# A convolution and a hard-swish layer on one core: the last convolution tap one unit earlier, a level-two sum moved from VectorE to GpSimd, and four ScalarE steps re-timed

## The chip, the core and the metric

The kernel runs on one core of a Trainium2 chip. The core has five engines that run their own instruction streams and wait for one another through semaphores: TensorE (PE in the profile; its weight loads are PEld), VectorE (DVE), ScalarE (ACT), GpSimd (POOL) and SyncE (SP), which here only issues DMAs. GpSimd issues DMAs as well, among them those that add to what is at the target. The metric is the device time of one execution in microseconds, and the time of the kernel before is the median of three runs.

## The reference

What is computed is a short causal convolution and, on its result, a two-layer network with a hard-swish between the layers, all in fp32:

```python
w = exp(weight - max(weight)); w = w / (sum(w) + 1e-9)      # (8 heads, 7 taps)
out = einsum('hk,bskhg->bshg', w, x_unf)                    # x: (8, 4096, 192), 7 taps back in time
x = out.reshape(32768, 192)
h = x @ w_in                                                # (192, 2048)
g = h * clip(h + 3.0, 0.0, 6.0) / 6.0
return g @ w_out                                            # (2048, 192)
```

## The kernel before

**Blocks.** The 32768 tokens are worked off in 32 blocks of 1024, each in two groups of 512. Block 0 is done in another way while the weights are prepared; blocks 1 to 31 are alike, and each runs `first_layer` (lines 499 to 570) and then `second_layer` (623 to 911). The last block differs a little: it has no convolution to prepare, and its output is finished in halves.

**The first layer.** The product with w_in is made from three parts (HIGH, LOW, MIX) of the operands, each rounded to a faster matmul format. There are 16 units n: 8 chunks of the 2048 inner columns for each of two groups. A unit takes one of four slots of two PSUM banks. `begin(n)` issues the HIGH and LOW matmuls, 12 of them, and ScalarE multiplies the slot by 4097 (L523; for unit 15 one half is done by ScalarE in L526 and the other by VectorE in L527). `end(n)` issues the 6 MIX matmuls, ScalarE makes the clipped factor (L302, "gate input") and VectorE multiplies it with the slot into the tile g (L306, "gate"). Then the slot is free: the HIGH matmuls of unit n + 4 wait for the gate of unit n. The order on TensorE is end(n), begin(n + 2), except that begin(15) stands before end(13). Two matmuls run side by side in the upper and the lower half of the array.

**Work between the units.** `jobs` puts work on VectorE behind given units, the taps of the convolution for the next block among it (L1053, one of 7 taps over 128 x 1536 elements; five of them fall here). The tile x is read by these taps alone, so that the load of the next one (L82 and L83, SyncE's queue, in the program behind the first layer) waits for the last tap.

**The second layer** multiplies g, as a 2 x 2 matrix of blocks A11, A12, A21, A22, by w_out with seven products in place of eight. The sums that it needs are written over the blocks or into the tile S3 (`s` in the profile):

| name | what | made by | where |
|---|---|---|---|
| S3 | A11 - A21, in pairs of chunks 0 to 3 | "third sum": GpSimd for pairs 0 and 1, VectorE for 2 and 3 | L414, S3 |
| S1 | A21 + A22, in the same pairs | `add_pair`: accumulating DMA on GpSimd's queue, behind its third sum | L573, over A21 |
| S2 | S1 - A11 | VectorE, half at a time | L414, over A11 |
| S4 | A12 - S2, in four pairs | `negative`: ScalarE writes -S2 (L576), a DMA of GpSimd's queue adds A12 | over S3 |

For the last 32 of the 96 output columns, products 1, 5, 2 and 4 are themselves split in the same manner ("level two", `small` products 1 to 7). The sums for these are made by `small_sums` (L605): `shared` from A11, `sums4` from A22 (z in the profile, which names other tiles of that kind z too), `sums2` from A12 and s5 from S1. Sum 3 is a difference of two blocks, sum 2 takes sum 3, and sum 4 takes sum 2. The first of each is made by a copying DMA (L556, L559) and an accumulating one.

**What sets the order.** TensorE's work in the second layer is written as four streams, one for each quarter of the array's columns, which run side by side. Each matmul gets a step of its stream's clock: a plain one of 512 tokens costs two steps, one of 256 tokens (level two) one, and each stream is 80 steps long. Copies, sums and DMAs for the other engines are given due times with `do(t, ...)`, put at t - 0.5. All are sorted by time and issued in that order; ties keep the order of the code. TensorE executes strictly in order, so that a matmul of one stream that waits holds all four. Stream 3 begins with product 1's level two, and at step 4 `fill(2)` brings the first two chunks of product 5, which read S1's first pair. Stream 2 has product 4's level two (`level_two(4, ...)`, order 1, then 6, 2, 7, 5, 4, 3) with chunks of product 7 ("c7", T3 times S3) in between. The level-two results are held in pieces of PSUM with names: A2, E2, C2, B2, D2 for product 2, and `chains` for the others; between two products that build on one another ScalarE copies a piece (L745 to L750, and L814 to L824 by due time; a copy called through `do` shows as L652). `fold` adds the pieces on VectorE.

Of the kernel before, what the change touches and what calls it, by code (L numbers as in the profile page):

```python
# [25 lines left out]
def kernel(  # L26
# [8 lines left out]
    nc = tc.nc  # L35
# [19 lines left out]
    NP = NC // 2  # L55
# [32 lines left out]
    for base, dma in ((0, nc.scalar), (D2, nc.sync)):  # L88
        dma.dma_start(
            out=w_sb[base : base + D2],  # L90
            in_=weight.unsqueeze(1).to_broadcast([H, GJ, KC]),
# [126 lines left out]
    for n in range(AHEAD):  # L218
# [8 lines left out]
        out=e_sb[:], in0=w_sb[:], in1=mx[:].to_broadcast([P, KC]), op=ALU.subtract  # L227
# [46 lines left out]
    A11, A21, A12, A22 = (g4[:, :, j] for j in range(4))  # L274
# [26 lines left out]
    def relu(r6, h):  # L301
        nc.scalar.activation(r6, h, ACT.Relu, bias=half[:], scale=1.0 / 6.0)  # L302

    def gate(g_, h):

        nc.vector.scalar_tensor_tensor(  # L306
            out=g_, in0=g_, scalar=1.0, in1=h, op0=ALU.min, op1=ALU.mult
        )
# [46 lines left out]
    every = range(NP)  # L355
# [90 lines left out]
    def rows(q):  # L446
        return slice(q * QS, (q + 1) * QS)
# [24 lines left out]
    def r32(ap):  # L472
        return ap.bitcast(F32R)
# [16 lines left out]
    y_own, y_other, pools, sums4 = [], [None], [], []  # L490
# [8 lines left out]
    def first_layer(i, jobs):  # L499

        slots = {}

        def both(n):
            return psum[:, 2 * slots[n] : 2 * slots[n] + 2]

        def mms(n, part, start=False, stop=False):
            group, c = divmod(n, NP)
            for s in range(K3):
                for k in range(2):
                    r = slice(k * D2, (k + 1) * D2)  # L510
                    nc.tensor.matmul(  # L511
                        out=psum[:, 2 * slots[n] + k], lhsT=r32(w_in_parts[part][r, c, s]),
                        rhs=r32(y_other[0][r, part, s] if group else y_own[part][r, s]),
                        start=start and s == 0, stop=stop and s == K3 - 1,
                        skip_group_check=True,
                    )

        def begin(n):
            slots[n] = free_slots.pop(0)
            mms(n, HIGH, start=True)  # L520
            mms(n, LOW)
            if n + 1 < count:
                nc.scalar.mul(both(n), both(n), 4097.0)  # L523
            else:
                lower, upper = (psum[:, 2 * slots[n] + k] for k in range(2))
                nc.scalar.mul(lower, lower, 4097.0)  # L526
                nc.vector.tensor_scalar(  # L527
                    out=upper, in0=upper, scalar1=4097.0, scalar2=None, op0=ALU.mult
                )

        def end(n):
            group, c = divmod(n, NP)
            mms(n, MIX, stop=True)
            to = g4[:, c, 1:3] if group else g4[:, c, 0::3]
            relu(to, both(n))
            gate(to, both(n))
            free_slots.append(slots[n])

        count = 2 * NP
        begin(0)  # L540
        begin(1)
        for job in jobs.get(-1, ()):
            job()
        for n in range(count):
            if n == count - 3:
                begin(n + 2)
            end(n)
            if n < count - 3:
                begin(n + 2)
            for job in jobs.get(n, ()):  # L550
                job()
            if n < NP and n % 2:
                small_sums(shared, A11, (3, 2, 4), nc.gpsimd, every[n - 1 : n + 1])
            if n in (3, NP - 1):
                r = slice(n - 3, n + 1)
                nc.sync.dma_start(out=four_parts(shared[:, r])[0], in_=four_parts(A11[:, r])[2])  # L556
            if n == NP - 1:
                sums4[:] = [pools[0].tile([P, NP, N], F32, name="z4", tag="own")]
                nc.sync.dma_start(out=four_parts(sums4[0])[0], in_=four_parts(A22)[2])  # L559
                small_sums(sums4[0], A22, (3,), nc.gpsimd)  # L560
                adding(four_parts(shared)[0], four_parts(A11)[3])
            if n == NP + 1:
                third_sum(0)
                add_pair(0)
                adding(four_parts(sums4[0])[0], four_parts(A22)[3])
            if n == NP + 2:
                small_sums(sums4[0], A22, (2,), nc.vector)
            if n == NP + 3:
                third_sum(1)
                add_pair(1)  # L570

    def adding(out, x):
        nc.gpsimd.dma_start(out=out, in_=x, accum_op=ALU.add)  # L573
# [5 lines left out]
    def pair_of(p):  # L579
        return slice(2 * p, 2 * p + 2)  # L580

    def third_sum(p, engine=nc.gpsimd):
        g_sums(engine, (3,), every[pair_of(p)], 2)

    def add_pair(p):
        adding(S1[:, pair_of(p)], A22[:, pair_of(p)])
# [4 lines left out]
    def four_parts(x):  # L591
        return [x[:, c::2, t] for t in halves for c in range(2)]

    def small_sums(to, x, which, engine=nc.gpsimd, r=every):

        r = slice(r[0], r[-1] + 1)
        x11, x12, x21, x22 = four_parts(x[:, r])
        s1, s2, s3, s4 = four_parts(to[:, r])
        forms = {
            1: (s1, x21, x22, ALU.add), 2: (s2, x22, s3, ALU.subtract),  # L600
            3: (s3, x11, x21, ALU.subtract), 4: (s4, x12, s2, ALU.subtract),
        }
        for n in which:
            o, p, q, op = forms[n]
            engine.tensor_tensor(out=o, in0=p, in1=q, op=op)  # L605
# [17 lines left out]
    def second_layer(i, between):  # L623
        last = i + 1 == NB
        ours = [free_slots.pop(0) for _ in range(3)]
        x_, b, y_, c, a, _ = (psum[:, 2 * n + k] for n in ours for k in range(2))
# [4 lines left out]
        copy = nc.scalar.copy  # L631
# [3 lines left out]
        first, second, third, fourth = (rows(q) for q in range(4))  # L635
# [5 lines left out]
        A2, E2, C2, B2, D2 = f[first, lo], f[second, hi], h[first, lo], h[second, hi], h[third, hi]  # L641
# [5 lines left out]
        def put(j, cost, fn):  # L647
            streams[j].append((clock[j], fn))
            clock[j] += cost

        def do(t, fn, *args, **kw):
            streams[3].append((t - 0.5, lambda: fn(*args, **kw)))  # L652
# [7 lines left out]
        def plain(j, bank, n, q, chunks, start=False):  # L660
            x, w = prod[n]
            x = S3 if x is None else x
            for k, ch in enumerate(chunks):
                put(j, 2, lambda ch=ch, k=k: matmul(
                    j, bank[rows(j)], w_out[:, ch, w, q * QS : (q + 1) * QS], x[:, ch],
                    start and k == 0,
                ))
# [57 lines left out]
        def p2(r, t):  # L725
            return late["p2"][r, t]
# [13 lines left out]
        p4 = Fourth()  # L740
# [50 lines left out]
        p3(1)  # L791

        level_two(4, lambda: p4, (1,), 2)
        plain(2, c, 7, 2, every[:2], True)
        level_two(4, lambda: p4, rest, 2)
        plain(2, c, 7, 2, every[2:])
        plain(2, b, 6, 2, every)
        small(2, 3, D2, False, 2)
        p3(2)
# [15 lines left out]
            do(20 if t == hi else 16, copy, out=p4[third, t], in_=b[first, t])  # L815
        do(16, copy, out=p1[third], in_=b[second])
        do(20, copy, out=B2, in_=A2)
        do(32, copy, out=C2, in_=B2)
        do(32.2, copy, out=D2, in_=B2)
        do(32, copy, out=a[fourth], in_=a[second])  # L820
        do(40, lambda: copy(out=p2(second, hi), in_=C2))
        do(48, copy, out=a[second], in_=a[fourth])
        do(44, lambda: copy(out=p2(first, lo), in_=A2))
# [15 lines left out]
        do(32, fold_with, p1)  # L839
        do(35, small_sums, s5, S1, (3, 2), nc.vector)  # L840
        do(35.5, g_sums, nc.vector, (2,), every[4:], 4)
        do(32.5, fold_with, p4, 2)
        do(36, copy, out=b[m], in_=p1)
        do(21, last_sum, sums2, A12)
        do(36, small_sums, s5, S1, (1, 4), nc.vector)
        for n, t in zip(range(0, NP, 2), (34, 39, 48.3, 50.5)):
            do(t, negative, slice(n, n + 2))
        do(45.5, lambda: copy(out=late["p7"], in_=c[m]))
        do(60.2, lambda: add(late["u3"], b[m], late["p7"]))
# [83 lines left out]
    with tc.manual_schedule():  # L933
# [4 lines left out]
            out=c_sb[:], in0=e_sb[:], in1=sm[:].to_broadcast([P, KC]), op=ALU.mult  # L938
# [15 lines left out]
        for _ in range(3):  # L954

            nc.tensor.matmul(
                out=psum[:, b], lhsT=zeros[:, 0:P], rhs=zeros[:], start=True, stop=True
# [58 lines left out]
        n = 3  # L1016
# [92 lines left out]
        left = []  # L1109
        taps = conv[2:]  # L1110
        for i in range(1, NB):
            jobs = {n: [tap] for n, tap in zip((-1, 1, 3, 5, 8), taps)}
            jobs[-1] = left + jobs.get(-1, [])
            first_layer(i, jobs)
            def begin_conv():
                x_tiles[i + 2] = load_x(i + 2)
                conv[:] = conv_jobs(i + 2)

            between, conv = [], []
            if i + 1 < NB:  # L1120
                between += [(37, split_high), (57, split_low), (70, split_mix)]
                between += [
                    (t, lambda n=n: swap_parts(nc.gpsimd, (n,)))
                    for n, t in ((HIGH, 69), (LOW, 69), (MIX, 71))
                ]
            if i + 2 < NB:
                between += [(1, begin_conv), (58, lambda: conv[0]()), (62, lambda: conv[1]())]
            left = second_layer(i, between)
            taps = conv[2:]
# [33 lines left out]
```

## Time and profile before

| | |
|---|---|
| median of 3 runs | 2321.71 us (2321.39 to 2323.81) |
| the profiled execution | 2322.07 us |
| its span, first to last instruction | 2320.3 us |
| TensorE matmuls busy | 2223.4 us (96%) |
| VectorE | 2028.5 us (87%) |
| ScalarE | 1718.9 us (74%) |
| GpSimd | 1175.4 us (51%) |
| one block in the middle, from its first L511 to the next one's | 71.18 us (1026.52 to 1097.70) |
| its first layer (L511) | 35.92 us (1026.52 to 1062.44) |
| the last block's first layer | 34.44 us (2238.50 to 2272.94) |

Times inside the run are microseconds from the span's start. A line of the order of time reads: start, duration, engine, line of the kernel, operation, output tile and input tiles, shape, how many in a row; in brackets stands how long the engine had been idle and who released it. Matmuls overlap, so a stretch of them counts as busy even where each one takes longer than its own work; a gap is real. A line of the waits reads: who waited for whom, total us, how often, longest. A DMA's line ends with the size and the time from issue to landing; the two queues named are `software_dynamic`, which GpSimd issues, and `hardware_dynamic`, which SyncE issues (packets, MB, share of the 16 DMA engines' time).

### The profile page before, as it was taken

How to read it: one execution, taken by the hardware profiler on the slowest of the kernel's cores; microseconds unless marked ns; L12 is line 12 of the kernel's file. 1: busy time of each engine (PE TensorE's matmuls, PEld its weight loads, DVE VectorE, ACT ScalarE, POOL GpSimd, SP SyncE). 2: the span in 40 equal slices, each digit the busy share in tenths (PEclk: the TensorE clock that was granted, in tenths of full speed). 3: DMA queues.
4: the chain of work that ended last, by engine and by line, in shares of the span. 5: the costliest groups of instructions: out<-in, count | busy, mean ns of one | idle time of the engine just before them, and what ended most of it. 6: DMA issues, size and time to landing. Idle time of an engine off the chain costs nothing.

```text
span 2320.3 us, 55454 instructions
## 1 busy us (share of the span) xinstructions
PE 2223.4 (96%) x22984; PEld 1494.0 (64%) x22984; DVE 2028.5 (87%) x1890; ACT 1718.9 (74%) x2360; POOL 1175.4 (51%) x1033
## 2 busy tenths in 40 slices
PE   9999999999999999999999999999999999999998
PEld 5466666666666666666666666666666666666664
DVE  8889898888888898888898888888888888889876
ACT  7568777687776777776877767777678777687775
POOL 2445554455544555444555445554455554455533
PEclk9999999999999999999999999999999999999999
DMA  6388878878879788788787888787977878878777
GB/s 150 74 145 152 158 146 149 168 142 154 153 146 167 140 153 158 143 162 152 147 157 151 151 163 143 151 158 141 167 144 150 158 145 157 156 146 156 141 150 114
DMA packets 386541, 345.71 MB, mean 149 GB/s; under 512 B 213969, under 2 KB 298449, under 8 KB 386289
## 3 DMA queue, kind: packets, MB, share of 16 engines
q0 software_dynamic: 131344, 250.72, 60.8%
q1 hardware_dynamic: 253704, 91.18, 18.2%
q8 instruction: 180, 2.95, 0.5%
q14 instruction: 73, 0.59, 0.1%
q10 hardware_dynamic: 1240, 0.27, 0.1%
HBM read 31.72 MB, written 25.17 MB: 25 GB/s over the span
## 4 chain that ended last, share of the span: by engine, by line
PE 57%; ACT 24%; issue 9%; DVE 9%; DMA 1%; POOL 0%; DVEq 0%; ACTq 0%; SPq 0%; POOLq 0%
PE psum L655 43%; ACT g L302 13%; PE psum L511 10%; ACT psum L523 8%; DVE g L306 4%; DVE z L605 3%; PE psum L296 2%; PE psum L341 2%; ACT psum L652 2%; DVE y L1053 1%; ACT z L750 0%; ACT shared L750 0%; DMA s<-g 0%; DVEq L605 0%; DMA x<-in_x_dram 0%
## 5 line engine op out<-in xcount | busy, mean ns | idle before, releaser
L655 PE MATMUL psum<-g,w_out 128*32 128x512 f32 (+1 forms) x5968 | 883.7, 504 | 2.9 <-DMA g<-g 2.9
L306 DVE SCALAR_TENSOR_TENSOR g<-g,psum 128x1024 f32<-128x1024 f32 (+1 forms) x528 | 613.3, 1183 | 97.8 <-ACT g L302 97.5
L655 PE MATMUL psum<-s,w_out 128*32 128x512 f32 (+1 forms) x3024 | 663.0, 586 | 1.3 <-DMA s<-g 1.3
L511 PE MATMUL psum<-y_other,w_in 64*128 64x512 f32 x4464 | 534.5, 390 | 71.8 <-DVE g L306 71.8
L302 ACT ACTIVATE g<-psum,half 128x1024 f32<-128x1024 f32 (+1 forms) x528 | 565.0, 1087 | 6.2 <-PE psum L511 5.5
L523 ACT ACTIVATE psum<-psum 128x1024 f32<-128x1024 f32 x465 | 468.7, 1008 | 98.4 <-PE psum L511 95.8
L511 PEld LDWEIGHTS psum<-y_other,w_in 64*128 64x128 f32 x4464 | 413.8, 184 | 182.4 <-DVE g L306 97.6
L511 PE MATMUL psum<-y_own,w_in 64*128 64x512 f32 x4464 | 523.3, 389 | 0.0
L655 PEld LDWEIGHTS psum<-g,w_out 128*32 128x32 f32 x5968 | 357.7, 110 | 228.9 <-issue 82.2
L511 PEld LDWEIGHTS psum<-y_own,w_in 64*128 64x128 f32 x4464 | 414.0, 184 | 117.1 <-issue 26.0
L1053 DVE SCALAR_TENSOR_TENSOR y<-x,c_sb,y 128x1536 f32<-128x1536 f32 x186 | 392.6, 2111 | 1.5 <-ACT y L1051 1.3
L605 POOL TENSOR_TENSOR shared<-g,shared 128x256 f32<-128x256 f32 x248 | 313.6, 1265 | 89.6 <-DVE g L306 57.6
L655 PE MATMUL psum<-g,w_s 128*32 128x256 f32 x1488 | 286.0, 379 | 0.0
L573 POOL DMA_DIRECT2D s<-g x124 | 149.4, 1264 | 261.9 <-ACT s L576 255.2
L655 PE MATMUL psum<-z,w_out 128*32 128x256 f32 x992 | 235.1, 380 | 13.8 <-ACT psum L652 13.8
L655 PE MATMUL psum<-z,w_s 128*32 128x256 f32 x992 | 235.8, 381 | 0.0
L655 PEld LDWEIGHTS psum<-s,w_out 128*32 128x32 f32 x3024 | 187.1, 110 | 63.6 <-issue 26.9
L573 POOL DMA_DIRECT2D g<-g x124 | 149.3, 1218 | 143.7 <-DVE s L414 124.2
L414 POOL TENSOR_TENSOR s<-g 128x1024 f32<-128x1024 f32 x62 | 167.0, 2694 | 47.0 <-DVE g L306 47.0
L414 DVE TENSOR_TENSOR g<-g 128x2048 f32<-128x2048 f32 x62 | 141.9, 2288 | 43.9 <-issue 43.9
L605 POOL TENSOR_TENSOR shared<-g 128x256 f32<-128x256 f32 x124 | 91.9, 741 | 170.4 <-DVE g L306 170.4
L573 POOL DMA_DIRECT2D z<-g x62 | 94.6, 1526 | 152.3 <-ACT z L576 141.5
(114 smaller groups left out, 2771.4 us busy)
## 6 DMA issues: line engine op xcount, KB each, us to landing
y_other<-y_own POOLq DMA_DIRECT2D x180, 384.0 KB, 8.0
g<-g POOLq DMA_DIRECT2D x124, 512.0 KB, 6.8
s<-g POOLq DMA_DIRECT2D x124, 512.0 KB, 5.3
z<-g POOLq DMA_DIRECT2D x62, 512.0 KB, 7.1
out_dram<-shared SPq DMA_DIRECT2D x378, 64.0 KB, 4.6
x<-in_x_dram SPq DMA_DIRECT2D x53, 388.5 KB, 7.7
shared<-g SPq DMA_DIRECT2D x62, 256.0 KB, 2.5
z<-g SPq DMA_DIRECT2D x31, 512.0 KB, 3.3
```

Of the source, the lines that this page charges most:

```text
L296: nc.tensor.matmul(out=psum[:, b], lhsT=w[r], rhs=src, start=start, stop=stop, skip_group_check=onto,)
L302: nc.scalar.activation(r6, h, ACT.Relu, bias=half[:], scale=1.0 / 6.0)
L306: nc.vector.scalar_tensor_tensor(out=g_, in0=g_, scalar=1.0, in1=h, op0=ALU.min, op1=ALU.mult)
L341: lambda p=p: nc.tensor.matmul(out=bank[j * QS : (j + 1) * QS, tokens], lhsT=w_out[:, p, w, cols], rhs=x[:, p, tokens], start=(first and p ...
L414: engine.tensor_tensor(out=o[:, r], in0=a[:, r], in1=b[:, r], op=op)
L511: nc.tensor.matmul(out=psum[:, 2 * slots[n] + k], lhsT=r32(w_in_parts[part][r, c, s]), rhs=r32(y_other[0][r, part, s] if group else y_own[ ...
L523: nc.scalar.mul(both(n), both(n), 4097.0)
L573: nc.gpsimd.dma_start(out=out, in_=x, accum_op=ALU.add)
L605: engine.tensor_tensor(out=o, in0=p, in1=q, op=op)
L652: streams[3].append((t - 0.5, lambda: fn(*args, **kw)))
L655: nc.tensor.matmul(out=out, lhsT=w, rhs=x, start=start, stop=True, tile_position=(0, j * QS), skip_group_check=True,)
L1053: jobs.append(lambda k=k: nc.vector.scalar_tensor_tensor(out=y[:], in0=x[:, :, k : k + N], scalar=c_sb[:, k : k + 1], in1=y[:], op0=ALU.mu ...
```

## The change

It has four parts.

- The fifth of the taps in the first layer stands behind unit 7 instead of unit 8 (line 1112).
- Sum 2 of `sums4`, 128 x 1024 elements, leaves VectorE behind unit 10 and is made by GpSimd behind unit 11, after third sum 1 and ahead of S1's second pair. In stream 2, four chunks of c7 in place of two stand ahead of the rest of product 4's level two, whose first product (6) reads that sum; the others of c7 follow it, so the whole level two ends four steps later.
- ScalarE's copy of B2 into C2 goes from 32 to 31.9, ahead of the level-two copies of that step; the copy of a's second rows into its fourth rows goes from 32 to 28. The copy into D2 stays at 32.2.
- The fold of product 4 goes from 32.5 to 36.3, the second `negative` from 39 to 40.5, and `split_high`, which writes HIGH for the next block's first layer into the buffer that held `sums4`, from 37 to 40.

```diff
@@ first_layer
                 third_sum(0)
                 add_pair(0)
                 adding(four_parts(sums4[0])[0], four_parts(A22)[3])
-            if n == NP + 2:
-                small_sums(sums4[0], A22, (2,), nc.vector)
             if n == NP + 3:
                 third_sum(1)
+                small_sums(sums4[0], A22, (2,), nc.gpsimd)
                 add_pair(1)
@@ second_layer
         level_two(4, lambda: p4, (1,), 2)
-        plain(2, c, 7, 2, every[:2], True)
+        plain(2, c, 7, 2, every[:4], True)
         level_two(4, lambda: p4, rest, 2)
-        plain(2, c, 7, 2, every[2:])
+        plain(2, c, 7, 2, every[4:])
@@ second_layer
         do(20, copy, out=B2, in_=A2)
-        do(32, copy, out=C2, in_=B2)
+        do(31.9, copy, out=C2, in_=B2)
         do(32.2, copy, out=D2, in_=B2)
-        do(32, copy, out=a[fourth], in_=a[second])
+        do(28, copy, out=a[fourth], in_=a[second])
@@ second_layer
-        do(32.5, fold_with, p4, 2)
+        do(36.3, fold_with, p4, 2)
...
-        for n, t in zip(range(0, NP, 2), (34, 39, 48.3, 50.5)):
+        for n, t in zip(range(0, NP, 2), (34, 40.5, 48.3, 50.5)):
             do(t, negative, slice(n, n + 2))
@@ the loop over blocks
-            jobs = {n: [tap] for n, tap in zip((-1, 1, 3, 5, 8), taps)}
+            jobs = {n: [tap] for n, tap in zip((-1, 1, 3, 5, 7), taps)}
...
-                between += [(37, split_high), (57, split_low), (70, split_mix)]
+                between += [(40, split_high), (57, split_low), (70, split_mix)]
```

## The prediction

> **What bounds the kernel now.** I read first the page's engine shares, then the table of who waited for whom, then the order of time of one block in the middle of the run, engine by engine, and last the DMA issues. TensorE's matmuls fill the span, so I looked for what interrupts them:
>
> ```profile
> PE 2223.4 (96%) x22984; PEld 1494.0 (64%) x22984; DVE 2028.5 (87%) x1890; ACT 1718.9 (74%) x2360; POOL 1175.4 (51%) x1033
> PE psum L511 <- DVE g L306: 71.8, 61, 1.6
> PE psum L655 <- ACT psum L652: 13.8, 31, 0.5
> PE psum L655 <- DMA g<-g: 2.9, 1, 2.9
> PEld psum L655 <- DMA g<-g: 5.9, 8, 3.8
> ```
>
> The last four are waits: who, for whom, us in total, times, longest. Three places per block: two waits for VectorE's gates (61 = 2 x 30 + 1), one for ScalarE's copies (31), and a DMA that holds TensorE a little in eight blocks. Now the block from 1026.52 to 1097.70 (71.18 us), TensorE, then VectorE, then GpSimd (start, us, what):
>
> ```profile
> 1044.43 8.32 PE L511 MATMUL psum<-y_other,w_in 64*128 64x512 f32 x72
> 1054.10 3.71 PE L511 MATMUL psum<-y_other,w_in 64*128 64x512 f32 x30 [1.34 <-DVE g L306]
> 1058.80 3.71 PE L511 MATMUL psum<-y_other,w_in 64*128 64x512 f32 x30 [0.99 <-DVE g L306]
> 1062.44 2.34 PE L655 MATMUL psum<-g,w_out 128*32 128x512 f32 x26
> 1078.61 0.40 PE L655 MATMUL psum<-z,w_out 128*32 128x256 f32 x1 [0.45 <-ACT psum L652]
> ```
>
> ```profile
> 1043.08 1.81 DVE L1053 SCALAR_TENSOR_TENSOR y<-x,c_sb,y 128x1536 f32<-128x1536 f32 x1
> 1049.20 3.71 DVE L1053 SCALAR_TENSOR_TENSOR y<-x,c_sb,y 128x1536 f32<-128x1536 f32 x1
> 1052.83 2.34 DVE L306 SCALAR_TENSOR_TENSOR g<-g,psum 128x1024 f32<-128x1024 f32 x2
> 1055.09 2.52 DVE L605 TENSOR_TENSOR z<-g,z 128x1024 f32<-128x1024 f32 x1
> 1057.53 2.34 DVE L306 SCALAR_TENSOR_TENSOR g<-g,psum 128x1024 f32<-128x1024 f32 x2
> ```
>
> ```profile
> 1043.30 2.20 POOL L605 TENSOR_TENSOR shared<-g,shared 128x256 f32<-128x256 f32 x1 [0.37 <-POOL shared L605]
> 1048.90 2.39 POOL L605 TENSOR_TENSOR z<-g 128x1024 f32<-128x1024 f32 x1
> 1051.22 1.34 POOL L573 DMA_DIRECT2D shared<-g  x1
> 1054.13 2.39 POOL L414 TENSOR_TENSOR s<-g 128x1024 f32<-128x1024 f32 x1 [1.57 <-DVE g L306]
> 1056.83 1.21 POOL L573 DMA_DIRECT2D g<-g  x1 [0.30 <-POOL s L414]
> 1058.83 2.95 POOL L414 TENSOR_TENSOR s<-g 128x1024 f32<-128x1024 f32 x1
> ```
>
> A convolution tap costs 1.81 us, but the one behind unit 8 took 3.71: it began while GpSimd ran its 2.39 us sum, and was done 1.6 us after that ended (1051.29). The sum on VectorE (2.52) stood likewise against GpSimd's third sum (to 1056.52); alone such a sum takes 1.22. Reversed, at 1043.30, GpSimd's 0.74 us sum stretched to 2.20 behind a tap. So these two-input instructions exclude each other, and the first one runs through. Each delay makes two gates late, units 9 and 11, and TensorE stops, as unit n+4 takes unit n's PSUM slot.
>
> **The change, step by step.** *Tap to unit 7, sum off VectorE.* The tap starts behind gate 7 at 1047.16, with GpSimd waiting, and ends at 1048.97. Gate 8 ends at 1050.1; unit 12's matmuls need it at 1050.55 (they run now without a gap). Gate 9 ends at 1051.3 (needed 1052.60), gate 11, straight behind ScalarE's gate input (1054.15), at 1055.35; it is needed no sooner than 1056.0. Both waits go. The last block, which has no tap, prices this: its first layer takes 34.44 us (2238.50 to 2272.94) with one wait of 1.16; less that and 0.1 of restart, 33.18. The second layer then starts at 1026.52 + 33.18 = 1059.70, not 1062.44: 2.74 earlier.
>
> *What is late next* is S1's first pair, A21 + A22 by an accumulating DMA on GpSimd's queue. Stream 3 reads it at step 4; a step is (35.26 - 0.45) / 80 = 0.435 us, so it was needed at 1064.18 and would be needed at 1061.44. The DMA was issued at 1056.83 and took 6.5 us (first line), so it landed 0.9 us ahead; in the seven of 30 blocks where it took 7.7, TensorE's weight loads do wait. GpSimd's queue does not get earlier: behind the tap its last two small sums end at 1050.40 (0.22 + 2.20 + 0.08 + 0.74 after 1047.16) instead of 1048.94, its 2.39 us sum follows, the first DMA issue starts at 1052.68 (1051.22 now), and third sum and second DMA issue stand 4.10 behind that, as in the last block (2263.22 to 2267.32): 1056.78. What changes is the traffic before it. The x tile is released by the last tap, so x loads are issued at 1049.0, not 1052.94. Now they run between the two additions (lines 2 and 3, stretches 1053 to 1056.9 and 1057 to 1060; last column is the share of 16 DMA engines):
>
> ```profile
> g<-g POOLq DMA_DIRECT2D x1, 512.0 KB, 6.5
> q0 software_dynamic: 514, 0.52, 107.3%
> q1 hardware_dynamic: 378, 0.74, 106.8%
> g<-g POOLq DMA_DIRECT2D x1, 512.0 KB, 5.2
> ```
>
> After, they have the idle engines from about 1051 on, and with the 5.5 us that x took on idle engines they land by 1055, about when the first addition begins to move (1052.68 + 1.8). On SyncE's queue nothing stands behind them before the stores at 1091. The fourth line is the same addition in block 30, which loads no x: 5.2 us, and 5.2 in the last block. I take that: 1056.78 + 5.19 + 0.04 = 1062.01. Ends: the shortest of all additions in the trace, 5.0, and 6.5, if x still stands ahead. Step 4 moves from 1064.18 to 1062.01: **2.17 us x 30 = 65.1**.
>
> The Trainium skill, page "DMA: Bandwidth & Descriptors", section "Anatomy of one DMA — SWDGE (gpsimd) path", puts such a transfer at 2.0 us plus bytes over 436e3: as an estimate 3.2 us for 512 KB. By that the pair would be there before step 4, and the gates alone would set the time, 2.74 x 30 = 82.2. No row agrees: the shortest here is 5.0.
>
> *The sum on GpSimd.* Third sum 1 ends 4.96 after the second DMA issue (2267.32 to 2272.28), at 1061.74; the new sum takes 2.33 (its sister: 2260.89 to 2263.22) and ends at 1064.07. Needed first at step 12, 1062.01 + 8 x 0.435 = 1065.5; without the four steps' delay it would be 1063.75, too early. The c7 chunks 2 and 3 that fill those steps need third sum 1 at step 8, 1063.75: there. At 2.95, the longest row, it still fits. Queued behind it: the issue of S1's second pair, 2.3 later (1064.4), landing near 1069.6; VectorE's S2 wants it at 1071.6 (step 26). VectorE's third sums, ready at 1062.96 behind gate 15, wait for the port until 1064.07; TensorE wants them at step 28. Cost: nothing. In the last block the second pair is waited for already (the 2.9 line): issued 2.3 later, without the 6.8 us it took behind another addition but 5.1, it lands **0.6** later; at worst 2.3.
>
> *Copies.* TensorE waits 0.45 at step 36 until C2, a's fourth rows (0.56) and D2 are copied, all behind step 32. C2 now goes first, and a's copy, whose product ends at step 28, runs in ScalarE's idle 1.77. Done by step 35: **13.8** in all gone. At worst none.
>
> *The rest.* Level two of product 4 ends four steps later, so its fold goes from 32.5 to 36.3, which frees VectorE 0.85 us earlier for S1's sums; split_high goes from 37 to 40, as its buffer holds sums that are read until 36. ScalarE has then no ready work from about step 38 to 40, and its negatives end near step 56.5 instead of 55.7: 0.33 us. Their DMAs are the tightest end of the block (weight loads wait for s in seven blocks): 7 x 0.33 = **2.3** lost; between 0 and 10.
>
> Sum: 65.1 + 13.8 - 0.6 - 2.3 = 76.0. The profiled execution took 2322.07 (span 2320.3 and 1.8 around it), 0.36 over the median of 2321.71, so 2321.7 - 76.0 = **2246**. Own range, 5.0 to 5.6 us of landing and copies gone or half gone: 2240 to 2265.
>
> **Rivals.** *x still in the way*: both transfers overlap and the pair takes 6.5. Step 4 gains 0.90: 27.0 + 13.8 - 2.9 = 37.9, **2284**. For it: x took up to 9.3 us in some blocks. Against: four microseconds of head start.
>
> *The pair no longer binds*: 82.2 + 13.8 - 2.9 = 93.1, **2229**. Only 0.57 us of wait separates it from my forecast.
>
> *Slower: the new sum loses the port.* If third sum 1 ends more than 1.2 us late, VectorE's two third sums and the next sum of A12 go first (1062.96 to 1066.5), and the sum ends at 1068.9. Step 12, today at 1067.66, comes 1.24 late: 1.24 x 30 - 13.8 = 23.4 lost, **2345**. It decides once the sum ends past 1068.1. For it: the stretched rows above. Against: third sum 1 ends 4.96 behind the issue in this block and the last alike. The Trainium skill, page "SBUF — State Buffer", section "SBUF: two separate sides", calls the shared port an exclusive lock for whoever starts first; the stretched rows agree.
>
> *The gain is absorbed later*, by the negatives' additions that product 3 needs at steps 64 to 76. The last of them lands 6.5 us after its issue in this block and 8.3 in others; a TensorE that comes earlier by that difference and waits there gives back 1.8 x 30 = 54: **2300**. For it: the seven waits for s. Against: their issues follow TensorE's steps, so they come earlier with it.
>
> **Chances.** Forecast 0.57, no binding 0.17, x in the way 0.13, absorbed 0.07, slower 0.05, no change 0.01. Under 0.2% (4.6 us) a measurement of this kernel can't tell a change. Faster 0.94, same 0.01, slower 0.05. The range leaves out the slower and absorbed cases, and widens 2229 and 2284 by a little: 2224 to 2288.
>
> **What would show it.** Tap behind unit 7 at 1.8 us; no L511 wait for L306; first layers near 33.2; TensorE waiting some 0.6 for DMA g<-g at step 4; no wait for L652; GpSimd's second z sum near 2.4, without a wait for z behind it. I am wrong if the addition still takes 6.5 us or if TensorE waits for POOL z or DMA s.

## The result, and the profile after

The changed kernel takes 2405.69 us (median of 4 runs, 2405.57 to 2405.95) against 2322.76 for the kernel before, run beside it: a ratio of 1.0357, with a 95% interval of 1.0339 to 1.0375. It is 83 us slower; 76 us faster was forecast. The profiled execution took 2405.64 us, its span 2403.9.

The engine shares and TensorE's largest waits in the kernel after (who, for whom, us in total, times, longest). One line of code is gone ahead of these places, so that L655 of before is L654 here, and L746 is L745:

```profile
PE 2277.8 (95%) x22984; PEld 1502.9 (63%) x22984; DVE 1942.0 (81%) x1859; ACT 1718.2 (71%) x2360; POOL 1291.7 (54%) x1064
```

```profile
PE psum L654 <- DVE z L458: 27.8, 31, 0.9
PE psum L654 <- ACT z L745: 25.5, 31, 1.0
PE psum L654 <- ACT z L747: 22.5, 31, 0.7
PE psum L654 <- ACT psum L746: 17.0, 32, 1.9
PE psum L654 <- ACT z L748: 12.6, 31, 0.4
PE psum L654 <- DMA g<-g: 6.5, 7, 4.6
PE psum L654 <- DMA s<-g: 5.8, 12, 2.0
```

The three waits of before that the change was aimed at, two for gates in L511 and one for L652, are gone from this table. Five new ones stand in it, each in all 31 blocks: four for a copy by ScalarE (L745 to L748, the copies of level two) and one for a fold by VectorE (L458). The order of time of one block, TensorE alone, shows where they fall:

```profile
1058.47 16.04 PE L511 MATMUL psum<-y_own,w_in 64*128 64x512 f32 x138
1076.39 15.12 PE L511 MATMUL psum<-y_other,w_in 64*128 64x512 f32 x132
1098.12 0.38 PE L654 MATMUL psum<-z,w_s 128*32 128x256 f32 x1 [0.48 <-ACT psum L746]
1100.89 0.40 PE L654 MATMUL psum<-g,w_out 128*32 128x256 f32 x1 [0.81 <-ACT z L745]
1103.65 0.40 PE L654 MATMUL psum<-z,w_out 128*32 128x256 f32 x1 [0.41 <-ACT z L748]
1106.40 0.40 PE L654 MATMUL psum<-z,w_s 128*32 128x256 f32 x1 [0.72 <-ACT z L747]
1110.98 0.40 PE L654 MATMUL psum<-z,w_out 128*32 128x256 f32 x1 [0.90 <-DVE z L458]
```

The first layer runs through. The five waits stand in the first half of the second layer, at nearly equal distances: 2.77, 2.76, 2.75, and then 4.58. By the steps of the streams they are at 12, 16, 20, 24 and 32. The two layers of this block as sums, first and second (us; busy time and instructions of PE, PEld, DVE, ACT, POOL; granted clock, DMA share, GB/s), after and then before:

```profile
1058.47:1091.44 32.97, 32.97 (x293) 26.83 (x289) 27.59 (x25) 30.85 (x32) 23.72 (x19) 1.00 0.73 157
1091.44:1131.77 40.33, 37.01 (x434) 20.41 (x432) 32.22 (x32) 22.69 (x42) 16.29 (x14) 1.00 0.84 138
```

```profile
1026.52:1062.44 35.92, 33.59 (x292) 26.68 (x289) 32.09 (x27) 30.87 (x32) 25.32 (x21) 1.00 0.76 156
1062.44:1097.70 35.26, 34.81 (x434) 19.70 (x432) 30.95 (x32) 22.73 (x42) 11.36 (x12) 1.00 0.89 150
```

The first layer won 2.95 us and the second lost 5.07, with 434 matmuls of TensorE in both. That is the whole result: over the run, 30 first layers win 30 x 2.95 = 88.5 and the last block's wins 1.5; the 30 second layers lose 5.38 each on the mean (35.37 to 40.75), 161.4; and the stretch behind the last first layer grows from 47.31 to 59.58, 12.3. 161.4 + 12.3 - 88.5 - 1.5 = 83.7, and the two profiled executions differ by 83.6.

The parts that the change moved did what was forecast of them. VectorE and GpSimd in the same block:

```profile
1079.12 1.81 DVE L1052 SCALAR_TENSOR_TENSOR y<-x,c_sb,y 128x1536 f32<-128x1536 f32 x1
1088.72 1.21 POOL L572 DMA_DIRECT2D g<-g  x1 [0.30 <-POOL s L414]
1090.29 3.39 POOL L414 TENSOR_TENSOR s<-g 128x1024 f32<-128x1024 f32 x1
1092.65 3.37 POOL L604 TENSOR_TENSOR z<-g,z 128x1024 f32<-128x1024 f32 x1
```

The tap takes 1.81 us, not 3.71. S1's first pair is issued 30.25 us behind the block's start (30.26 forecast), and the DMA issues of that moment show its size and landing:

```profile
g<-g POOLq DMA_DIRECT2D x1, 512.0 KB, 5.2
```

That is the 5.2 us that the forecast took, not the 6.5 of before. The lines of GpSimd's third sum and new sum overlap by 1.03 us; from the end of the third sum the new one takes 2.34. It is done at 1096.02, 37.55 behind the block's start, as forecast, and nobody waits for it.

### The profile page after: what moved, and what is told of

Same layout as the page of the kernel before. It is cut to its first block, busy times and chain, and to the rows that moved or that the text cites. A ratio compares the mean times of both kernels' runs of the same rounds, so it can differ in the third digit from the quotient of the medians.

```text
span 2403.9 us, 55514 instructions
## 1 busy us (share of the span) xinstructions
PE 2277.8 (95%) x22984; PEld 1502.9 (63%) x22984; DVE 1942.0 (81%) x1859; ACT 1718.2 (71%) x2360; POOL 1291.7 (54%) x1064
## 3 DMA queue, kind: packets, MB, share of 16 engines
q8 instruction: 180, 2.95, 0.5%
## 5 line engine op out<-in xcount | busy, mean ns | idle before, releaser
L654 PE MATMUL psum<-g,w_out 128*32 128x512 f32 (+1 forms) x5968 | 931.0, 506 | 34.2 <-ACT z L745 25.5
L654 PE MATMUL psum<-s,w_out 128*32 128x512 f32 (+1 forms) x3024 | 800.4, 591 | 5.9 <-DMA s<-g 5.8
L511 PE MATMUL psum<-y_own,w_in 64*128 64x512 f32 x4464 | 523.4, 389 | 0.0
L654 PEld LDWEIGHTS psum<-g,w_out 128*32 128x32 f32 x5968 | 354.8, 109 | 266.5 <-issue 75.6
L511 PE MATMUL psum<-y_other,w_in 64*128 64x512 f32 x4464 | 516.0, 386 | 0.0
L511 PEld LDWEIGHTS psum<-y_own,w_in 64*128 64x128 f32 x4464 | 413.5, 184 | 117.7 <-issue 26.0
L511 PEld LDWEIGHTS psum<-y_other,w_in 64*128 64x128 f32 x4464 | 418.1, 184 | 87.8
L604 POOL TENSOR_TENSOR shared<-g,shared 128x256 f32<-128x256 f32 x248 | 357.2, 1441 | 88.8 <-DVE g L306 57.5
L654 PE MATMUL psum<-g,w_s 128*32 128x256 f32 x1488 | 341.0, 380 | 0.4 <-ACT psum L744 0.4
L1052 DVE SCALAR_TENSOR_TENSOR y<-x,c_sb,y 128x1536 f32<-128x1536 f32 x186 | 335.2, 1802 | 1.5 <-ACT y L1050 1.4
L654 PE MATMUL psum<-z,w_out 128*32 128x256 f32 x992 | 205.2, 381 | 40.3 <-DVE z L458 27.8
L654 PE MATMUL psum<-z,w_s 128*32 128x256 f32 x992 | 204.5, 380 | 37.5 <-ACT z L747 22.5
L654 PEld LDWEIGHTS psum<-s,w_out 128*32 128x32 f32 x3024 | 197.9, 109 | 62.5 <-issue 14.8
L414 POOL TENSOR_TENSOR s<-g 128x1024 f32<-128x1024 f32 x62 | 195.5, 3153 | 0.0
L572 POOL DMA_DIRECT2D g<-g x124 | 180.1, 1466 | 17.9 <-POOL s L414 9.1
```

Of the source, the lines that this page charges most:

```text
L414: engine.tensor_tensor(out=o[:, r], in0=a[:, r], in1=b[:, r], op=op)
L511: nc.tensor.matmul(out=psum[:, 2 * slots[n] + k], lhsT=r32(w_in_parts[part][r, c, s]), rhs=r32(y_other[0][r, part, s] if group else y_own[ ...
L654: nc.tensor.matmul(out=out, lhsT=w, rhs=x, start=start, stop=True, tile_position=(0, j * QS), skip_group_check=True,)
L1052: jobs.append(lambda k=k: nc.vector.scalar_tensor_tensor(out=y[:], in0=x[:, :, k : k + N], scalar=c_sb[:, k : k + 1], in1=y[:], op0=ALU.mu ...
```

## The experiments

Where a run was repeated its median and range are given; the others are single runs, beside which the kernel before took 2322.4 to 2323.8 us in three groups of runs.

**The theory.** Level two of product 1 (stream 3, rows 96 to 127) and of product 4 (stream 2, rows 64 to 95) hold their pieces in the same two banks: `chains` puts A and E in x_, and B and C in y_, for both. The pieces do not overlap, but the waits of this kernel go by the whole bank. Each product writes one bank, and behind each but 4 a copy reads that bank: 6 writes y_, 2 x_, 7 y_, 5 x_, 4 y_, 3 y_. In step with each other, both streams write y_, then both write x_ while the copies read y_, and so on: never the same bank. Four steps apart, one stream writes the very bank that the other's copy reads. Going through the six products with a lag of four gives a collision at steps 12, 16, 20, 24, and at 32 with the fold of p1, which reads B; none at 28. Those are the five waits. The copies of one of them, ScalarE in the order of time of the kernel after:

```profile
1100.10 0.34 ACT L746 COPY psum<-psum 32x256 f32<-32x256 f32 x1 [2.12 <-PE psum L654]
1100.47 0.37 ACT L745 COPY z<-psum 32x256 f32<-32x256 f32 x1
```

At step 16 ScalarE makes two copies, product 4's behind its 6 and product 1's behind its 2 (L745, into p1); the second ends at 1100.84, and TensorE's matmul of 1100.89 starts behind it. The rival was that the new sum, or the DMAs behind it, delays level two whatever the distance of the streams.

**Back in step.** From the kernel after; the rest of the change stays:

```diff
-        plain(2, c, 7, 2, every[:4], True)
+        plain(2, c, 7, 2, every[:2], True)
         level_two(4, lambda: p4, rest, 2)
-        plain(2, c, 7, 2, every[4:])
+        plain(2, c, 7, 2, every[2:])
```

> The changed kernel with product 4's level two put back beside product 1's (two chunks of c7 ahead of it, six behind), everything else as changed. Bank theory (a product that writes one piece of a PSUM bank waits until ScalarE's or VectorE's read of another piece of the same bank is done; with a lag of four steps this happens at five step boundaries, 5.1 us a block): the five waits for copies and for the fold are gone, the second layer falls from 40.3 to about 35 us, plus up to 1.2 us because the new sum on GpSimd is now needed at step 8; 2240 to 2275 us. Rival (the re-timed copies, fold, split and negatives make the loss): the second layer stays near 40 us and the time within 1% of 2405.

Measured: 2302.94 us. The five waits are gone; the largest of TensorE that are left:

```profile
PE psum L654 <- ACT psum L744: 9.8, 31, 2.2
PE psum L654 <- DMA s<-g: 8.7, 12, 2.1
```

That settles the place, the four steps, and 103 us with it. But the kernel stays 28 us above the upper end of what was expected, and a wait for L744 has come in, which is taken up below.

**Eight steps instead of four.** Six chunks of c7 ahead (`every[:6]`, `every[6:]`), the fold of product 4 at 40.3 and `split_high` at 44:

> The changed kernel with a lag of eight steps instead of four: six chunks of c7 ahead of product 4's level two, its fold at 40.3 and split_high at 44. Bank theory: with eight steps both level twos are again in the same bank at the same time at four of the six boundaries, and only two collisions are left (step 28 with a copy, step 32 with a copy and the fold of product 1): about 2.3 us a block instead of 5.1, second layer near 37 us, time near 2305 us (2280 to 2330). Rival (what costs is that the two level twos are apart at all, so that ScalarE has to serve copies at more boundaries): as slow as with four steps or slower, 2400 us or more.

Measured: 2318.51 us. Among TensorE's waits one line is of this kind; the other collision, expected at step 28, shows in the weight loads alone:

```profile
PE psum L654 <- DVE z L458: 25.3, 31, 0.8
PEld psum L654 <- ACT shared L748: 9.1, 31, 0.3
```

Twice the delay costs far less than the single one. A cost that grew with the delay is out; the parity of the banks is what counts.

**Four steps, other banks.** The kernel after with its lag, but product 4's pieces in the opposite banks. The fold of p4 goes ahead of the sums that stood before it (36.05, the sums from 36.1 to 36.2), so that it is not late:

```diff
         chains = {
-            j: [bank[rows(j), t] for bank in (x_, y_) for t in halves] for j in (2, 3)
+            j: [bank[rows(j), t] for bank in banks for t in halves]
+            for j, banks in ((2, (y_, x_)), (3, (x_, y_)))
         }
```

> The changed kernel, lag of four steps kept, but product 4's level two uses the two banks in the other order (pieces A and E in the bank of unit 13, B and C in that of unit 12), and its fold stands ahead of S1's sums on VectorE. Bank theory: by the step list only one collision is left (step 28, product 1's third against the copy of product 4's E), about 1 us; and piece A now waits at step 0 for gate 13, about 1 us. Second layer near 37 us, time near 2300 us (2275 to 2330). Rival (being apart costs): unchanged or slower, 2400 us or more.

Measured: 2276.89 us, 128.8 less than the kernel after, with the same lag and the same sum on GpSimd. (The earlier fold may have a share in this; the runs on the fold, below, show what a late one can cost.) No matmul waits for a copy any more, and the one collision that was expected, at step 28, shows in the weight loads:

```profile
PE psum L655 <- DVE g L306: 6.1, 31, 0.5
PE psum L655 <- DMA g<-g: 3.9, 2, 3.4
PEld psum L655 <- ACT shared L748: 10.5, 31, 0.3
```

The new first line belongs to the swap: product 4's first piece now lies in y_, which the first layer's unit 13 has just left, and TensorE waits for that unit's gate.

**The delay alone.** The kernel before with the four chunks ahead, the fold at 36.3 and `split_high` at 40; tap, sum and copies as before:

> The kernel before with the four-step delay alone: four chunks of c7 ahead of product 4's level two, and what has to follow it, its fold at 36.3 and split_high at 40. Tap, sum and copies as before. Bank theory: the same five collisions, 5.1 us in each of 31 blocks on top of the kernel before: near 2480 us (2450 to 2500), with first layers of 35.9 us unchanged. Rival (the delay costs only together with the earlier second layer): within 1% of 2322 us.

Measured: 2464.11 us, 140.3 more than before. The largest waits of its matmuls:

```profile
PE psum L511 <- DVE g L306: 71.3, 61, 1.6
PE psum L655 <- DVE z L458: 27.7, 31, 0.9
PE psum L655 <- ACT z L746: 23.2, 31, 1.0
PE psum L655 <- ACT z L748: 22.4, 31, 0.7
PE psum L655 <- ACT z L749: 12.6, 31, 0.4
```

The rival is gone: the sum is on VectorE here, and four of the five waits stand beside the first layer's of before. The fifth, at step 12 (here for L747), holds matmuls three times only, 1.7 us, and weight loads 32 times, 21.7 us. The wait for L652 doesn't show either, though its copies are timed as before; TensorE comes to step 36 later here.

How much each wait costs is not its gap. This table, worked out from the traces, compares how far TensorE is behind the kernel before just ahead of each step: the start of the last matmul that belongs to an earlier step, counted from the second layer's first (median over 30 blocks, us later; 80 is the last matmul of all):

```
step          8     12     16     20     24     28     32     36     40     56     80
after       .41    .39   1.29   2.37   3.46   4.42   4.43   5.58   4.52   4.87   5.51
lockstep    .40    .95    .94    .95    .95    .94    .95   1.16    .30   1.10   2.07
swapped     .83   1.00    .99   1.01   1.01    .99   1.65   1.67    .74    .99   1.21
```

In the kernel after each of the five waits sets TensorE back by 0.9 to 1.2, 5.2 from step 12 to 36, while the gaps are 0.41 to 0.90, 3.32 together. In the kernel with the banks swapped 0.66 is lost behind step 28, where weight loads wait for the expected copy and for one more that is late on ScalarE (`z`, L748, 14.3 us in 31). At 40 the kernel after gets 1.06 back; the wait of before at step 36, which it does not have, is 0.61 of that by the run with the copies alone, and the other 0.45 are open, so that the five waits cost 4.7 to 5.2 together.

**The rest of the change without the delay.** The kernel before with the tap behind unit 7, the two copies re-timed and the sum on GpSimd, but ahead of third sum 1, as without the delay it is needed at step 8; fold, `negative` and `split_high` as before:

```diff
-            if n == NP + 2:
-                small_sums(sums4[0], A22, (2,), nc.vector)
             if n == NP + 3:
+                small_sums(sums4[0], A22, (2,), nc.gpsimd)
                 third_sum(1)
                 add_pair(1)
...
-        do(32, copy, out=C2, in_=B2)
+        do(31.9, copy, out=C2, in_=B2)
...
-        do(32, copy, out=a[fourth], in_=a[second])
+        do(28, copy, out=a[fourth], in_=a[second])
...
-            jobs = {n: [tap] for n, tap in zip((-1, 1, 3, 5, 8), taps)}
+            jobs = {n: [tap] for n, tap in zip((-1, 1, 3, 5, 7), taps)}
```

> The kernel before with the tap behind unit 7, the two re-timed copies, and the sum on GpSimd ahead of third sum 1 instead of behind it, so that no delay of product 4's level two is needed; fold, split_high and negatives as before. If the delay and the later fold are all that made the change slow: first layer 33.0 us, second layer 34.8 to 35.4 us, no wait for copies or folds, 30 x (71.2 - 68.1) = 93 us less than before: near 2230 us (2215 to 2250). If something else of the change costs too (the sum on GpSimd, or S1's later second pair): 2260 us or more.

Measured: 2239.0 us (2238.74 to 2240.52 in 4 runs), a ratio to before of 0.9637, interval 0.9621 to 0.9653. It beats both kernels. Shares and waits:

```profile
PE 2223.3 (99%) x22984; PEld 1573.8 (70%) x22984; DVE 1936.2 (86%) x1859; ACT 1721.3 (77%) x2360; POOL 1293.4 (58%) x1064
```

```profile
PE psum L654 <- DMA g<-g: 6.5, 6, 5.0
PE psum L654 <- DMA s<-g: 1.8, 1, 1.8
```

TensorE's share goes from 96% to 99% with its busy time unchanged. What is left of waits is mostly one of 5.0 us in the last block.

**The late fold.** The run back in step came out 28 us above its range, and it kept the fold of product 4 at 36.3. First the same with the sum ahead of third sum 1, so that against the last kernel only fold, `negative` and `split_high` differ:

> The changed kernel with product 4's level two beside product 1's again and the sum on GpSimd ahead of third sum 1; against the kernel named combo only fold (36.3), second negative (40.5) and split_high (40) are later. Bank theory: with the fold behind S1's sums on VectorE, ScalarE's copy into product 5's chain at step 48 waits for the fold's read of the same bank, and TensorE with it, about 1 us a block: some 30 us slower than combo, near 2260 us. Rival (these three only change ScalarE's order): within 10 us of combo.

Measured: 2303.76 us, 64.8 above the last kernel, where some 30 were expected. Then the fold by itself, from the last kernel:

```diff
-        do(32.5, fold_with, p4, 2)
+        do(36.3, fold_with, p4, 2)
```

> The kernel named combo with product 4's fold at 36.3 instead of 32.5 and nothing else. Bank theory: ScalarE's copy into product 5's chain (step 48) waits for the fold's read of the same bank, which now stands behind 7 us of sums on VectorE; TensorE waits 1.2 us for the copy, and the two last negatives behind it on ScalarE are late at steps 72 to 80, another 1 us: 2.1 us a block, 60 to 70 us more than combo, near 2303 us. Rival (split_high and the second negative made the late end): about 37 us more, near 2276 us, with no wait for DMA s.

Measured: 2301.91 us, 62.9 more than without this one line. TensorE's two largest waits, then VectorE, ScalarE and TensorE in the order of time:

```profile
PE psum L654 <- ACT psum L744: 26.4, 31, 2.2
PE psum L654 <- DMA s<-g: 9.6, 13, 1.4
```

```profile
1283.45 2.35 DVE L604 TENSOR_TENSOR g<-g 128x1024 f32<-128x1024 f32 x2
1286.27 0.42 DVE L458 TENSOR_TENSOR shared<-psum,shared 32x256 f32<-32x256 f32 x1
1286.78 0.34 ACT L744 COPY psum<-psum 32x256 f32<-32x256 f32 x1 [3.13 <-DVE shared L458]
1287.17 0.40 PE L654 MATMUL psum<-g,w_s 128*32 128x256 f32 x1 [1.24 <-ACT psum L744]
```

The same rule of the bank, one step removed. At 36.3 the fold stands behind 7.1 us of sums on VectorE (2.49, 2.28 and the 2.35 of the first line). It reads product 4's B in y_; ScalarE's first copy for product 5's level two writes product 5's B, in y_ too, and waits for the fold; product 5's 6 waits for that copy. By the measure of the table above, 1.1 of the 2.3 us that a block loses against the last kernel fall between steps 48 and 56, with this wait. Another 1.1 fall behind step 72, where weight loads now wait for a DMA into s in every block (22.7 us in 31; 2.3 in one without this line); the two `negative` behind the late copy on ScalarE, whose DMAs these are, were expected to do that. In the changed kernel no matmul waited for L744; TensorE came there 4.5 to 4.9 us later than in the kernel before, by the table, which would explain it.

**`split_high` and `negative`.** From the same kernel, `split_high` at 40 and the second `negative` at 40.5:

> The kernel named combo with split_high at 40 and the second negative at 40.5 and nothing else. Bank theory: within 15 us of combo (my prediction gave it 0.33 us in a few blocks). Rival (these two make the late end): about 30 us more, near 2270 us, TensorE waiting for DMA s at steps 72 to 80.

Measured: 2242.47 us, 3.5 more; the wait for DMA s comes 6 times instead of once. This is one run, in another group of runs, and 2.0 above the highest of the four, so the 3.5 are likely and not shown.

**The copies alone**, from the kernel before, with the two lines of `copy` of the diff above:

> The kernel before with ScalarE's two copies re-timed alone (C2 at 31.9, a's fourth rows at 28). The wait of 0.45 us at step 36 goes in every block: 31 x 0.45 = 14 us less, near 2309 us. If the copy at 28 holds ScalarE, or another copy is late in its place: 2320 us or more.

Measured: 2301.47 us, 21.7 less than before. The wait of 0.45 at step 36 is gone, and from step 40 on every block is 0.61 earlier.

**The tap alone**, from the kernel before:

> The kernel before with the tap behind unit 7 alone. The prediction's first term without the sum: the wait behind unit 9's gate goes, the one behind unit 11's stays as in the last block, first layer 34.4 us instead of 35.9: 30 x 1.5 = 45 us less, near 2278 us. If S1's first pair, which is added no earlier, held TensorE at step 4: 2290 us or more.

Measured: 2346.28 us, 23 more than before, where a gain was expected. Two waits have become one of 2.6 (TensorE; then VectorE and GpSimd just ahead of it):

```profile
1214.69 3.69 PE L511 MATMUL psum<-y_other,w_in 64*128 64x512 f32 x30 [2.58 <-DVE g L306]
```

```profile
1209.24 4.27 DVE L605 TENSOR_TENSOR z<-g,z 128x1024 f32<-128x1024 f32 x1
1209.51 2.90 POOL L414 TENSOR_TENSOR s<-g 128x1024 f32<-128x1024 f32 x1
```

With the tap out of the way, VectorE's sum and GpSimd's third sum start side by side, and the sum takes 4.27 instead of 2.52. So nothing is gained (first layer 35.85 in blocks at full clock, 35.92 before), and the 23 us lost lie in the blocks with half the clock, below.

**The sum alone** on GpSimd, ahead of third sum 1, tap behind unit 8:

> The kernel before with the sum on GpSimd alone, ahead of third sum 1; tap behind unit 8, copies as before. If each delay of VectorE made its own wait: the wait of 1.34 stays, that of 0.99 goes, first layer 34.8 us, 30 x 1.1 = 33 us less, near 2290 us. If the two trade places, as they did when the tap alone moved: no gain, 2315 to 2325 us.

Measured: 2310.89 us, 11.5 less than before. The second wait of the first layer is gone, the first stays, and the first layer takes 34.62:

```profile
PE psum L511 <- DVE g L306: 40.7, 30, 1.6
PE psum L654 <- DMA g<-g: 11.9, 12, 5.0
```

The parts do not add: in blocks at full clock the tap alone wins nothing, the sum alone 1.3 us of each first layer, both together 2.95.

**The last block.** From the kernel of 2239.0 us; in the last block only, the sum goes behind S1's second pair:

```diff
-                small_sums(sums4[0], A22, (2,), nc.gpsimd)
+                if i + 1 < NB:
+                    small_sums(sums4[0], A22, (2,), nc.gpsimd)
                 third_sum(1)
                 add_pair(1)
+                if i + 1 == NB:
+                    small_sums(sums4[0], A22, (2,), nc.gpsimd)
```

> The kernel named combo, but in the last block the sum on GpSimd stands behind S1's second pair, so that this pair is added 2.4 us earlier; TensorE waits 5.0 us for it there in combo, and its clock is halved for 6.8 us behind that wait. Expected: the wait falls to about 2.7 us and less of the half clock follows, 2 to 5 us less than combo, 2234 to 2237 us. If the half clock comes as before: 2236.5 or more.

Measured: 2237.33 us (2235.75 to 2238.59 in 4 runs), ratio 0.963, interval 0.9614 to 0.9647. The last block's wait is 3.76 instead of 4.99, where 2.7 was expected, and the clock is halved for 6.83 us there as in the other kernel. The two kernels' ranges do not quite part (2238.59 against 2238.74), and the two stood in different groups of runs, so 1.7 us is a likely gain and not a shown one.

## Why the prediction was wrong

- *Tap to unit 7, sum off VectorE*: right. First layers take 32.97 (33.18 forecast), no wait of the first layer for a gate is left, 2.95 us earlier for 2.74. The two had to go together, as the runs with one of them show. The 0.1 for a restart behind the last block's wait was too small: that wait of 1.16 was worth 1.48 (34.44 to 32.96).
- *What is late next*: right in kind. S1's first pair, issued as forecast, lands 5.2 us later, and binds a little: ahead of step 8 the second layer is 0.41 late (0.40 in the kernel of 2239.0 us), where 0.57 was forecast. It shows in the weight loads, which wait for a DMA into g 31 times, 30.4 us (8 times, 5.9 us before); matmuls wait for it only 7 times.
- *The sum on GpSimd*, "Cost: nothing": here the prediction failed. It priced the sum's arrival, GpSimd's queue and the port, and in the block shown the sum came as forecast. What it did not price is the other half of the step, product 4's level two moved by four steps against product 1's. It asked whether each operand would be there, and never whether the place that a product writes would be free. With the delay and its later fold and `split_high` alone that is 140.3 us, 4.5 a block; taken away with the fold's new time left in, 102.8; and swapping the banks, with the fold in time, wins back 128.8. It explains the loss: the first layers' gain was there, and this term turned it over.
- *Copies*: right by themselves, and too small: 21.7 us instead of 13.8. The gap was counted (0.45), and 0.61 a block is what its end brought. In the changed kernel they can't be credited: the run with the delay alone keeps the old copies and has no wait for L652 either.
- *The rest*: `split_high` and `negative` cost 3.5 us in one run (2.3 forecast). The fold's later time was counted as a relief for VectorE; by itself it costs 62.9. That was the second error, of the same kind, and in the changed kernel the first one hid it.
- *The last block*: 0.6 was forecast for S1's second pair; its wait for an addition into g grew from 2.9 to 4.6.
- None of the rivals came true. The slower one named the port, and no matmul of the kernel after waits for the new sum. Of the two signs of being wrong, the waits for DMA s did come (12, 5.8 us), but they are a small part of the loss.

The trace of before held the answer in one line. The matmul of 1078.61 waited 0.45 for L652, and it was read as waiting for three copies. Its own, C2, was done at 1077.62; the copy that ended at 1078.56, right ahead of it, was D2's, another piece of the same bank h. That pointed to a wait by bank.

With the two errors taken out, the kernel without the delay and the late fold, its sum ahead of third sum 1, takes 2239.0 us, and 2246 had been worked out. That it comes so near is in part luck: it leaves out the later `negative` and `split_high` too, its first layers and copies win more than forecast, and its second layers, which should have won the copies' 0.61, are 0.17 longer than before on the mean (35.54 against 35.37), more than the 0.57 of waiting for S1 accounts for; the last one loses 3.6.

The Trainium skill, page "PSUM — Partial Sum Buffer", section "PSUM bank collisions raise a hardware error", asks to guard PSUM by bank and quarter of 32 partitions, and calls a guard by bank alone "the simple version". The waits here follow the simple version, as the L458 and L745 to L748 rows show. By the finer rule these five would not be needed, the pieces being in different quarters. No run here shows that: the waits cannot be taken away by themselves, and it was not tried.

## What to carry to other kernels

When a chain of work is moved in time, list what it writes as well as what it reads, and who else is reading or writing in the same PSUM bank at the new time; two chains that alternate between two banks without trouble in step collided in five of six places once they were one product apart. A releaser in the trace that is not the producer of the waiting instruction's data is a sign of a place that is guarded as a whole. And of a bundle of edits, test each part also from the best kernel, since one error can hide another (the fold's 62.9 us).

## What the runs showed of the hardware

**A wait of 2.6 us can halve TensorE's clock.** In the run with the tap alone, about half of the blocks are 1.3 us or more longer than the others. Two blocks as sums, next to each other (columns as above), and then 0.4 us of the first, 2.2 us behind its wait:

```profile
751.60:824.05 72.45, 69.43 (x724) 47.49 (x721) 62.98 (x58) 53.61 (x73) 38.58 (x34) 0.98 0.81 150
824.05:895.20 71.15, 68.13 (x725) 46.48 (x722) 62.96 (x57) 53.62 (x73) 38.54 (x33) 1.00 0.83 153
```

```profile
786.00:786.40 0.40, 0.40 (x4) 0.30 (x4) 0.00 (x0) 0.00 (x0) 0.40 (x1) 0.50 1.22 179
```

In the wait that ended at 783.83 the granted clock fell to 0.50 at 783.29, and stayed there for 3.41 us; the 30 matmuls behind it took 5.02 us, against 3.69 behind the equal wait of another block (1214.69). The waits of 0.99 and 1.34 in the blocks of the kernel before never did this; that of the last block (2.9 to 5.0) did it in before, after and the kernel of 2239.0 us, but one of 2.95 in the run with the copies alone did not. The Trainium skill, page "TensorE: Matmul & The Clock Gate", section "What's actually happening", tells of a window of 3413 ns that runs freely and of half the clock after an idle one. The 3.41 us agree. But the wait of 2.6 us is shorter than that window, so a wait need not fill a whole one.

The trace of the run with the tap alone says which waits count. Its half-clock stretches (18 in all) begin whole multiples of 3.413 us apart, from 131.35 to 2343.18. Laid on that grid, 17 of its 32 waits of over 2 us have 1.95 us or more inside one window, and the clock is halved at that window's end each time; the other 15 have at most 1.85 inside one, and it never is. So here somewhere between 1.85 and 1.95 us of waiting inside one window of 3.413 was enough, and a longer wait that straddles two windows could pass.

**The gap that a trace shows is not the whole price of a wait.** The copies' gap of 0.45 was worth 0.61, the two gaps of 2.33 in the first layer 2.95, the 1.16 in the last block 1.48, and the five gaps of 3.32 us cost 4.7 to 5.2. Where the rest goes is open.
